# Attention and a gated convolution on one core: 1/z turned on VectorE, scaled values transposed, twelve more groups by DMA, another beginning and end

## The chip, the cores and the metric

The kernel runs on one core of a Trainium2 chip. The time is the device time of one execution in microseconds (us); three executions of the kernel before took 1075.22, 1075.74 and 1079.62 us, median 1075.74. The engines are named as in the profile: PE (TensorE), PEld (its weight loads), DVE (VectorE), ACT (ScalarE), POOL (GpSimd), SP (SyncE, which here only issues DMAs; SPq is its queue).

## The reference

Inputs are q of 4 x 12288 x 128, kv of 4 x 384 x 32 x 128 and a few matrices of 128 columns.

```python
kv_pool = kv.reshape(B, H // r, r, W // r, r, C).mean(axis=(2, 4))   # r = 4: 768 keys a batch
k = v = kv_pool.reshape(B, -1, C) @ w_sr
s = (q @ k.transpose(0, 2, 1)) / sqrt(C)
a = exp(s - s.max(-1)); a /= a.sum(-1) + 1e-09
x = a @ v
# gated convolution over x (5 taps, causal, per column)
gate = sigmoid(sum(conv_w[k] * shifted(x, k) for k in range(5)))
out = (gate * (x @ w_val)) @ w_out
```

All is float32. The matrices of the second half (w_val, w_out and the taps, one array w_moe) arrive as float64 and are turned into float32 bit by bit on DVE (14 steps, `load_moe`).

## The kernel before, in words

The host hands q, kv and the output over transposed, channels on partitions. The work is cut into 4 batches of 24 **groups** of 512 queries, and each group into four **tiles** j = 0 to 3 of 128 queries: 96 groups, 384 steps.

**Keys.** kv of a batch comes in 16 pieces of 128x768 (`load_kv`, L117) through a ring of AHEAD buffers. DVE sums each over its 4x4 blocks (`pool_kv`, L120). Two projections by w_sr (`project`, L133, 384 keys each) and three evictions (`split_keys`, L142, L143 on ScalarE, L146 on DVE) give a high part kh, a rest kl and the full vt. For the values, `column_scale` (L162 to L170) takes the largest value of each channel, makes a power of two of it and puts it on a diagonal matrix; `values` (L176) multiplies vt by this diagonal, which transposes and scales in one matmul, three tiles of 128 at a time, and L185 and L188 split the result into 16-bit vh and vl.

**One group.** A tile's score (`score`, L251) is the sum of three products kh·qh, kl·qh and kh·ql, each in two halves of 384 keys, in a pair of PSUM banks. There are three such pairs. DVE takes the row maximum (L257), ACT the exponential and its sum into a column of z (`expo`, L269), ACT the high 16-bit half of the result (`p_hi`, L316), DVE the low half (`p_lo`, L320), which is the last to read the banks. The tile must then be transposed for the product with the values. For tiles j < by_dma this is done by DMA_TRANSPOSE from SP (L324, two tiles at a time or one); for the others PE turns the float32 tile with six transposes back into its own banks (`turn`, L299) ahead of the two halves. by_dma is 3, but 4 in the even groups of the last batch. The 18 products with the values (L333, 16-bit) fill the av bank in four parts.

**1/z.** After the fourth tile ScalarE adds 1e-9 to the four sums (`norm_eps`, L273). A group later DVE takes the reciprocal (L276), PE transposes a 128x128 tile of which four columns count (`norm_turn`, L279, into the misc bank), DVE copies the four rows out (L286), one DMA stores them to DRAM (`norm_store`, L287, rd), and a second reads them back as one row on all 128 partitions (`norm_rows`, L292, rb). x is av times the power of two times rb (`g_x`, L350).

**After x.** Four taps and the sums run on POOL (L360, L369), the fifth tap on ACT (L358), the gate's tanh on ACT (L385), h on DVE (L394), and PE multiplies by w_val (L389) and w_out (L399).

**Order.** It is written by hand and nothing reorders it. In step (group, j) the program works on several groups: the scores one tile ahead, softmax of the current group `cur`, 1/z of `last` (one back), av of `avg` (two back), the convolution of `xg` (three back), the products of `mg` (four back), the store of `og` (five back). Preparing the next batch is dripped into groups 2 to 22 of the one before it and groups 0 and 1 of its own: pieces and poolings in groups 2 to 18, projections in 19 and 20, the column scale from 21, the values in the new batch's groups 0 and 1. After the last step an epilogue (L536 on) finishes the five groups in flight, written out line by line; there the convolution of the last two groups runs on DVE alone (`conv_dve`, L375, L377).

Of the kernel before, what the change touches and what calls it, by code (L numbers as in the profile page):

```python
# [17 lines left out]
GQ = 512  # L18
NT = GQ // P

# [6 lines left out]
def attn_moe_kernel(ctx, tc, qT, kvT, w_sr, w_moe, outT):  # L27
# [16 lines left out]
    AHEAD = 5  # L44
# [22 lines left out]
    zs = [const.tile([P, P], F32, name=f"z{i}") for i in range(3)]  # L67
# [55 lines left out]

    def key_tiles(st):
# [7 lines left out]
    def project(st, h, m):  # L132
        nc.tensor.matmul(m[:, :HALF], wsr, st["pool"][:, h * HALF:(h + 1) * HALF],  # L133
                         start=True, stop=True)
        st["m"] = m[:, :HALF]

    def split_keys(st, h):
        sl = slice(h * HALF, (h + 1) * HALF)
# [13 lines left out]
    def column_scale(st):  # L152
# [6 lines left out]
        st["diag"] = keys.tile([C, C], F32, name="diag", bufs=1)  # L159
# [9 lines left out]
            lambda: v.tensor_scalar_mul(out=st["diag"], in0=ident, scalar1=up.bitcast(F32)),  # L169
# [3 lines left out]
    def values(st, h, m):  # L173
        for j in range(HALF // P):
            k = h * HALF + j * P
            nc.tensor.matmul(m[:, j * P:(j + 1) * P], st["vt"][:, k:k + P], st["diag"],  # L176
                             start=True, stop=True)
        st["m"] = m[:, :HALF]
# [22 lines left out]
    def setup_steps(b, st):  # L201
# [10 lines left out]
        steps += [lambda h=h: project(st, h, misc()) or split_keys(st, h) for h in range(2)]  # L212
# [32 lines left out]
    def score(g, j):  # L245
        sl = slice(j * P, (j + 1) * P)
        kh, kl = g.st["kh"], g.st["kl"]
        s = bank_pair()
        for i, (a, k) in enumerate(((g.qh, kh), (g.qh, kl), (g.ql, kh))):
            for h in range(2):  # L250
                nc.tensor.matmul(s[:, h, :HALF], a[:, sl], k[:, h * HALF:(h + 1) * HALF],  # L251
                                 start=(i == 0), stop=(i == 2))
        g.s[j] = s[:, :, :HALF]
# [24 lines left out]
    def norm_turn(g, m):  # L278
        nc.tensor.transpose(m[:, :P], g.z, ident)  # L279
        g.rm = m[:NT, :P]  # L280

    def norm_store(g):

        r = small.tile([NT, P], F32, name="r")
        g.rd = dram.tile([NT, P], F32, name="rd")
        nc.vector.tensor_copy(out=r, in_=g.rm)  # L286
        nc.sync.dma_start(out=g.rd, in_=r)  # L287

    def norm_rows(g):
        g.rb = work.tile([C, GQ], F32, name="rb", bufs=3)  # L290
        row = g.rd.rearrange("(o j) p -> o (j p)", o=1)
        nc.sync.dma_start(out=g.rb, in_=row.broadcast_to([C, GQ]))  # L292
# [80 lines left out]
    def conv_dve(g, c0=0, c1=GQ):  # L373
# [61 lines left out]
    key_tiles(st)  # L435
    for i in range(AHEAD):
# [3 lines left out]
    g_qh(at(0))  # L440
    g_ql(at(0))
# [179 lines left out]
```

## Time and profile before

| | |
|---|---|
| three executions | 1075.22, 1075.74, 1079.62 us |
| profiled execution | 1078.68 us |
| its span | 1076.9 us, granted TensorE clock 0.996 |
| PE, DVE, ACT, POOL busy | 1038.4, 919.5, 903.7, 865.2 us |
| first and last sum of a group (L273) | 37.1 and 1050.4 us |
| queue of SP: kv, q, out, rb, rd, transposes | 64, 49, 51, 96, 96, 192 issues |

Busy time is the sum over an engine's instructions, with overlaps counted once. PE's matmuls are pipelined, so the durations of neighbours overlap; a price of one is better read from the starts. A row "a:b c, ..." of the windows gives the stretch in us, its length, and then for each engine its busy time and its count of instructions, the granted clock of PE, the busy share of the DMA engines and what they moved. In a row of the timeline the first number is the start, the second the duration; what stands in brackets is how long the engine sat idle ahead of it and what released it. Three numbers with slashes are minimum, median and maximum in ns.

### The profile page before, as it was taken

The page shows a single profiled execution, that of the slowest core. Times are in us where ns is not written, and L with a number is a line of the kernel's source. Part 1 is how long each engine was busy: PE and PEld are TensorE (multiplying, and loading weights), DVE is VectorE, ACT ScalarE, POOL GpSimd, SP SyncE. Part 2 cuts the span into 40 slices and gives each one's busy share as a digit, 9 for nine tenths or more (in the row PEclk, how much of TensorE's full clock was granted, in tenths as well). Part 3 has the DMA queues.
Part 4 walks back from the last instruction along what each step waited for, and adds up shares of the span by engine and source line. Part 5 has one row for each costly group of instructions (what it writes and reads, how often), then busy time and mean ns, then how long its engine had stood idle before and what let it go on. Part 6 is the DMA issues. An engine that isn't in the chain of part 4 may idle for free.

```text
span 1076.9 us, 16475 instructions
## 1 busy us (share of the span) xinstructions
PE 1038.4 (96%) x5102; PEld 706.5 (66%) x5102; DVE 919.5 (85%) x1290; ACT 903.7 (84%) x1659; POOL 865.2 (80%) x948
## 2 busy tenths in 40 slices
PE   1899999999999999999999999999999999999996
PEld 0666666666666666666676666666666666666663
DVE  6888989898888898988888989898888888888885
ACT  1788888888888888888888888888888988888882
POOL 0178888888888888888888888888887888888882
PEclk9999999999999999999999999999999999999999
DMA  7699999998889999999689999997899999999994
GB/s 285 115 237 215 214 225 234 200 192 190 182 186 234 226 222 224 220 214 188 156 182 221 248 216 219 235 218 177 174 203 191 200 209 218 206 194 212 201 178 120
DMA packets 505527, 220.25 MB, mean 205 GB/s; under 512 B 471520, under 2 KB 472288, under 8 KB 505440
## 3 DMA queue, kind: packets, MB, share of 16 engines
q1 hardware_dynamic: 505440, 219.20, 92.7%
q8 instruction: 41, 0.67, 0.2%
q14 instruction: 46, 0.38, 0.1%
HBM read 75.83 MB, written 25.36 MB: 94 GB/s over the span
## 4 chain that ended last, share of the span: by engine, by line
PE 89%; DVE 5%; ACT 2%; DMA 2%; issue 1%; POOL 0%; SPq 0%; DVEq 0%; ACTq 0%
PE s L251 36%; PE av L333 32%; PE m L389 7%; PE m L399 7%; PE s L299 5%; DMA kvt<-in_kv 2%; DVE nm L257 1%; PE m L279 1%; ACT s L269 1%; ACT hl L316 1%; DVE hl L320 1%; DVE pt L320 1%; DVE pool L120 0%; DVE x L350 0%; PE m L176 0%
## 5 line engine op out<-in xcount | busy, mean ns | idle before, releaser
L333 PE MATMUL av<-pt,vh 128*128 128x512 f16 x1140 | 387.1, 381 | 0.0
L369 POOL TENSOR_TENSOR sum<-sum,tap 128x512 f32<-128x512 f32 x282 | 360.3, 1278 | 22.1
L257 DVE TENSOR_REDUCE nm<-s 128x1 f32<-128x768 f32 x384 | 363.9, 948 | 2.8 <-PE s L251 2.8
L269 ACT ACTIVATE s<-s,nm 128x768 f32<-128x768 f32 x300 | 262.0, 873 | 88.7 <-DVE nm L257 80.0
L360 POOL TENSOR_SCALAR tap<-x,wm 128x512 f32<-128x512 f32 x376 | 253.4, 693 | 78.1 <-DVE x L350 76.8
L320 DVE SCALAR_TENSOR_TENSOR hl<-s,hl 128x768 f16<-128x768 f32 x300 | 284.8, 949 | 21.4 <-ACT hl L316 21.1
L251 PE MATMUL s<-kh,qh 128*128 128x384 f32 x768 | 252.9, 410 | 6.0 <-DVE hl L320 2.3
L316 ACT ACTIVATE hl<-s 128x768 f16<-128x768 f32 x300 | 243.0, 810 | 9.1
L333 PEld LDWEIGHTS <-vh 128*128 128x128 f16 x1164 | 113.5, 98 | 173.6 <-issue 81.5
L333 PE MATMUL av<-pt,vl 128*128 128x512 f16 x570 | 216.0, 379 | 0.0
L251 PE MATMUL s<-kh,ql 128*128 128x384 f32 x768 | 198.0, 339 | 0.0
L251 PE MATMUL s<-kl,qh 128*128 128x384 f32 x768 | 197.7, 338 | 0.0
L237 POOL TENSOR_TENSOR ql<-q,qh 128x512 fp32r<-128x512 f32 x96 | 122.0, 1271 | 93.3 <-ACT qh L233 92.5
L251 PEld LDWEIGHTS s<-kh,qh 128*128 128x128 f32 x768 | 132.4, 192 | 51.1 <-PE m L279 4.4
L251 PEld LDWEIGHTS s<-kl,qh 128*128 128x128 f32 x768 | 140.5, 189 | 0.5 <-DVE kl L146 0.5
L251 PEld LDWEIGHTS s<-kh,ql 128*128 128x128 f32 x768 | 139.8, 189 | 0.0
L394 DVE SCALAR_TENSOR_TENSOR h<-th,m 128x512 f32<-128x512 f32 x94 | 64.7, 688 | 69.0 <-PE m L389 63.4
L369 POOL TENSOR_TENSOR sum<-tap,tap 128x512 f32<-128x512 f32 x94 | 120.3, 1280 | 0.0
L350 DVE SCALAR_TENSOR_TENSOR x<-av,down,rb 128x512 f32<-128x512 f32 x95 | 71.3, 751 | 44.5 <-POOL ql L237 30.5
L333 PEld LDWEIGHTS <-vl 128*128 128x128 f16 x582 | 57.2, 98 | 76.6 <-issue 53.6
L399 PE MATMUL m<-h,wm 128*128 128x512 f32 x188 | 96.8, 597 | 1.2 <-DVE h L394 1.2
L389 PE MATMUL m<-x,wm 128*128 128x512 f32 x188 | 96.1, 592 | 0.0
(68 smaller groups left out, 1001.9 us busy)
## 6 DMA issues: line engine op xcount, KB each, us to landing
kvt<-in_kv SPq DMA_DIRECT2D x64, 384.0 KB
rb<-rd SPq DMA_DIRECT2D x96, 256.0 KB
q<-in_q SPq DMA_DIRECT2D x47, 512.0 KB
out<-o SPq DMA_DIRECT2D x46, 512.0 KB
pt<-hl SPq DMA_TRANSPOSE x192
rd<-r SPq DMA_DIRECT2D x96, 2.0 KB
out<-o SPq DMA_DIRECT2D x3, 256.0 KB
q<-in_q SPq DMA_DIRECT2D x2, 256.0 KB
```

The source lines that it names most:

```text
L237: nc.gpsimd.tensor_tensor(out=g.ql, in0=g.q, in1=g.qh.bitcast(F32), op=ALU.subtract)
L251: nc.tensor.matmul(s[:, h, :HALF], a[:, sl], k[:, h * HALF:(h + 1) * HALF], start=(i == 0), stop=(i == 2))
L257: nc.vector.tensor_reduce(out=nm, in_=g.s[j], axis=AX.XY, op=ALU.max, negate=True)
L269: nc.scalar.activation(out=halves(g.pf[j]) if on_pe(g, j) else g.s[j], in_=g.s[j], func=AF.Exp, bias=g.nm.pop(j), accum_out=g.z[:, j:j + 1])
L316: nc.scalar.activation(out=part(g, j, 0), in_=g.s[j], func=AF.Copy, scale=2.0 ** 15)
L320: nc.vector.scalar_tensor_tensor(out=part(g, j, 1), in0=g.s.pop(j), scalar=2.0 ** 15, in1=part(g, j, 0), op0=ALU.mult, op1=ALU.subtract)
L333: nc.tensor.matmul(out, g.st[v][:, k * P:(k + 1) * P], g.pt[:, j0:j1, a * NCH + k], start=(i == 0), stop=(i == len(AV_ORDER) - 1))
L350: nc.vector.scalar_tensor_tensor(out=g.x[:, HALO + c0:HALO + c1], in0=av, scalar=g.st["down"], in1=g.rb[:, c0:c1], op0=ALU.mult, op1=ALU.mult)
L360: eng.tensor_scalar(out=g.tap[k], in0=src, scalar1=w, scalar2=1.0, op0=ALU.mult, op1=ALU.mult)
L369: nc.gpsimd.tensor_tensor(out=s, in0=acc, in1=g.tap[k], op=ALU.add)
L389: nc.tensor.matmul(m, wval, g.x[:, HALO + c0:HALO + c1], start=True, stop=True)
L399: nc.tensor.matmul(m, wout, h, start=True, stop=True)
```

## The change

- **1/z.** z becomes 128x32. DVE takes the reciprocal and transposes it itself in 32x32 blocks into r of 128x32: each block of 32 queries leaves its four rows on partitions 0, 32, 64 and 96 on. Four DMAs of 4x32 store them in place of one of 4x128. Reciprocal and transpose now come behind the low half of the step, and PE and the misc bank have no part in it. `norm_store` and `norm_rows` take the queue as an argument.
- **Values.** The diagonal is gone. ScalarE multiplies vt by the power of two in place (128x768), and PE only transposes vt.
- **by_dma** is 4 also in groups 0, 18, 20 and 22 of the first three batches, the even ones that load no piece of keys.
- **Beginning.** w_moe is loaded first and converted by DVE first (before: dripped into the steps from the fourth on). AHEAD is 7. Pieces 0, 2, 4 and 6 are summed on POOL by four halvings each. The keys are projected in three parts (384, 288, 96 columns), each as soon as its pieces are there, in the misc bank. The first halves of the scores of tiles 0 to 2 are multiplied as soon as the first 384 keys are split.
- **End.** All of av of the last but one group comes first; rb of it is issued in step 2 of the last group, ahead of that group's transposes; rd and rb of the last group go through ScalarE's queue; the convolution of the last two groups has two of its taps on ACT (`conv_mixed`) and two adds more on DVE; products and outputs come in another order.

```diff
-    AHEAD = 5
+    AHEAD = 7
-    zs = [const.tile([P, P], F32, name=f"z{i}") for i in range(3)]
+    zs = [const.tile([P, BLOCK], F32, name=f"z{i}") for i in range(3)]
+    def pool_halving(st, i):
+        t = st.pop(("kv", i)).rearrange("c (k s) -> c k s", s=RR)
+        n = RR // 2
+        while n:
+            to = t[:, :, :n]
+            if n == 1:
+                to = st["pool"][:, i * PC:(i + 1) * PC].rearrange("c (k s) -> c k s", s=1)
+            nc.gpsimd.tensor_tensor(out=to, in0=t[:, :, :n], in1=t[:, :, n:2 * n], op=ALU.add)
+            t, n = to, n // 2
...
-            lambda: v.tensor_scalar_mul(out=st["diag"], in0=ident, scalar1=up.bitcast(F32)),
+            lambda: nc.scalar.activation(out=st["vt"], in_=st["vt"], func=AF.Copy,
+                                         scale=up.bitcast(F32)),
...
-            nc.tensor.matmul(m[:, j * P:(j + 1) * P], st["vt"][:, k:k + P], st["diag"],
-                             start=True, stop=True)
+            nc.tensor.transpose(m[:, j * P:(j + 1) * P], st["vt"][:, k:k + P], ident)
...
-    def norm_turn(g, m):
-        nc.tensor.transpose(m[:, :P], g.z, ident)
-        g.rm = m[:NT, :P]
-    def norm_store(g):
-        r = small.tile([NT, P], F32, name="r")
+    def norm_turn(g):
+        g.r = small.tile([P, BLOCK], F32, name="r")
+        nc.vector.transpose(out=g.r, in_=g.z)
+    def norm_store(g, eng):
         g.rd = dram.tile([NT, P], F32, name="rd")
-        nc.vector.tensor_copy(out=r, in_=g.rm)
-        nc.sync.dma_start(out=g.rd, in_=r)
+        for i in range(0, P, BLOCK):
+            eng.dma_start(out=g.rd[:, i:i + BLOCK], in_=g.r[i:i + NT])
...
+    def conv_mixed(g, c0, c1):
+        def product(k):
+            t = kvp.tile([C, PC * RR], F32, name="kvt", bufs=AHEAD)[:, :c1 - c0]
+            nc.scalar.activation(out=t, in_=g.x[:, k + c0:k + c1], func=AF.Copy,
+                                 scale=cwt[:, k:k + 1])
+            return t
+        late = [product(k) for k in range(TAPS - 2, TAPS)]
...
-        for k in range(1, TAPS):
+        for k in range(1, TAPS - 2):
             nc.vector.scalar_tensor_tensor(out=s, in0=g.x[:, k + c0:k + c1],
                                            scalar=cwt[:, k:k + 1], in1=s,
                                            op0=ALU.mult, op1=ALU.add)
+        for t in late:
+            nc.vector.tensor_tensor(out=s, in0=s, in1=t, op=ALU.add)
...
-            g.by_dma = 4 if b == B - 1 and i % 2 == 0 else 3
+            g.by_dma = 4 if i % 2 == 0 and (b == B - 1 or not 0 < i <= PIECES + 1) else 3
...
+    convert = load_moe()
     for i in range(AHEAD):
         load_kv(0, st, i)
...
+    by_pool = (0, 2, 4, 6)
+    ends = {PIECES // 2: slice(0, HALF), PIECES - 2: slice(HALF, NK - 2 * PC),
+            PIECES: slice(NK - 2 * PC, NK)}
+    for step in convert:
+        step()
+        if i in ends:
+            project(st, ends[i], misc())
+            high, low = split_keys(st, ends[i])
             high()
+        if i == PIECES // 2 + 1:
+            for j in first:
+                score(at(0), j, (0,))
...
-        if last and j == 0:
-            norm_reciprocal(last)
         if last and j == 1:
-            norm_store(last)
+            norm_store(last, nc.sync)
+        if cur is groups[-1] and j == 2:
+            norm_rows(last, nc.sync)
...
         if last and j == 0:
-            norm_turn(last, misc())
+            norm_reciprocal(last)
+            norm_turn(last)
-        if last and j == 3:
-            norm_rows(last)
+        if last and nxt and j == 3:
+            norm_rows(last, nc.sync)
```

Where instructions move, three places. **PE in the middle of the run**, from the last av matmul of a first part to the next score: L279 is z, L251 (after: L264) the score. Before:

```order
L333 MATMUL av<-pt,vh 128x512
L279 MATMUL m<-ident,z_101 128x128
L251 MATMUL s<-kh,qh 128x384 x2
L251 MATMUL s<-kl,qh 128x384 x2
L251 MATMUL s<-kh,ql 128x384 x2
```

After:

```order
L345 MATMUL av<-pt,vh 128x512
L264 MATMUL s<-kh,qh 128x384 x2
L264 MATMUL s<-kl,qh 128x384 x2
L264 MATMUL s<-kh,ql 128x384 x2
L411 MATMUL m<-x,wm 128x512
```

The score now follows av directly; the last row is the next product by w_val, which stood there before too.

**DVE in the same place**, from x of one group (L350, after L362) to the second low half of the next (L320, after L332). Before:

```order
L350 SCALAR_TENSOR_TENSOR x<-av,down,rb 128x512
L257 TENSOR_REDUCE nm<-s 128x1
L276 RECIPROCAL z_101<-z_101 128x4
L320 SCALAR_TENSOR_TENSOR pt<-s,pt 128x768
L257 TENSOR_REDUCE nm<-s 128x1
L286 COPY r<-m 4x128
L320 SCALAR_TENSOR_TENSOR hl<-s,hl 128x768
```

After:

```order
L362 SCALAR_TENSOR_TENSOR x<-av,down,rb 128x512
L269 TENSOR_REDUCE nm<-s 128x1
L332 SCALAR_TENSOR_TENSOR pt<-s,pt 128x768
L288 RECIPROCAL z_101<-z_101 128x4
L293 STREAM_TRANSPOSE r<-z_101 128x32
L269 TENSOR_REDUCE nm<-s 128x1
L332 SCALAR_TENSOR_TENSOR hl<-s,hl 128x768
```

The reciprocal has gone behind the low half, the transpose stands next to it, and nothing stands between the second row maximum and the second low half.

**SP in the last two groups**: rd and rb are the two steps of 1/z, L324 (after L336) the transposes of the last group's tiles. Before:

```order
L287 DMA rd<-r 4x128
L324 DMA_TRANSPOSE pt<-hl 128x24x128
L324 DMA_TRANSPOSE pt<-hl 128x12x128
L292 DMA rb<-rd 128x512
L287 DMA rd<-r 4x128
L413 DMA out<-o 128x1024
L292 DMA rb<-rd 128x512
```

After:

```order
L299 DMA rd<-r 4x32 x4
L304 DMA rb<-rd 128x512
L336 DMA_TRANSPOSE pt<-hl 128x24x128
L336 DMA_TRANSPOSE pt<-hl 128x12x128
L435 DMA out<-o 128x1024
```

The first rb has passed both transposes; the last rd and rb are no longer on this queue. In the middle of the run the order on SP is as before, with four rows of rd for one.

More of the change, by code (lines that the diff above doesn't have):

```diff
@@ L130, in key_tiles, with project, split_keys @@
         st["vt"] = keys.tile([C, NK], F32, name="vt", bufs=1)
-    def project(st, h, m):
-        nc.tensor.matmul(m[:, :HALF], wsr, st["pool"][:, h * HALF:(h + 1) * HALF],
-                         start=True, stop=True)
-        st["m"] = m[:, :HALF]
-    def split_keys(st, h):
-        sl = slice(h * HALF, (h + 1) * HALF)
+    def project(st, sl, m):
+        m = m[:, :sl.stop - sl.start]
+        nc.tensor.matmul(m, wsr, st["pool"][:, sl], start=True, stop=True)
+        st["m"] = m
+    def split_keys(st, sl):
         m = st.pop("m")
@@ L243, in halves, with score @@
         return a.rearrange("p (h k) -> p h k", h=2)
-    def score(g, j):
+    def score(g, j, part=range(2)):
         sl = slice(j * P, (j + 1) * P)
         kh, kl = g.st["kh"], g.st["kl"]
-        s = bank_pair()
+        if j not in g.s:
+            g.s[j] = bank_pair()[:, :, :HALF]
         for i, (a, k) in enumerate(((g.qh, kh), (g.qh, kl), (g.ql, kh))):
-            for h in range(2):
-                nc.tensor.matmul(s[:, h, :HALF], a[:, sl], k[:, h * HALF:(h + 1) * HALF],
+            for h in part:
+                nc.tensor.matmul(g.s[j][:, h], a[:, sl], k[:, h * HALF:(h + 1) * HALF],
                                  start=(i == 0), stop=(i == 2))
-        g.s[j] = s[:, :, :HALF]
     def row_max(g, j):
@@ L439, in attn_moe_kernel @@
     nc.sync.dma_start(out=wsr, in_=w_sr)
-    g_qh(at(0))
-    g_ql(at(0))
+    first = range(3)
+    by_pool = (0, 2, 4, 6)
+    ends = {PIECES // 2: slice(0, HALF), PIECES - 2: slice(HALF, NK - 2 * PC),
+            PIECES: slice(NK - 2 * PC, NK)}
     low = None
-    for i in range(PIECES):
-        if i + AHEAD < PIECES:
-            load_kv(0, st, i + AHEAD)
-        if i == 3:
-            convert = load_moe()
-        pool_kv(st, i)
-        if i == 3 * PIECES // 4:
-            low()
-        if i % (PIECES // 2) == PIECES // 2 - 1:
-            h = 2 * i // PIECES
-            project(st, h, bank_pair()[:, 0])
-            high, low = split_keys(st, h)
+    for step in convert:
+        step()
+    for i in range(1, PIECES + 1):
+        if i - 1 + AHEAD < PIECES:
+            load_kv(0, st, i - 1 + AHEAD)
+        (pool_halving if i - 1 in by_pool else pool_kv)(st, i - 1)
+        if low and i - 1 in ends:
+            low()
+        if i == PIECES // 2:
+            g_qh(at(0))
+            g_ql(at(0))
+        if i in ends:
+            project(st, ends[i], misc())
+            high, low = split_keys(st, ends[i])
             high()
+        if i == PIECES // 2 + 1:
+            for j in first:
+                score(at(0), j, (0,))
     low()
@@ L541, in attn_moe_kernel, with pair_of @@
     cuts = ((0, half), (half, GQ))
-    def bank():
-        return bank_pair()[:, 0]
+    def pair_of(width):
+        both = bank_pair()
+        return both[:, 0, :width], both[:, 1, :width]
+    for i in range(NT):
+        av_part(n2, i)
     norm_reciprocal(n1)
-    av_part(n2, 0)
-    norm_turn(n1, misc())
+    norm_turn(n1)
+    norm_store(n1, nc.scalar)
     n4.th = g_tanh(n4.gate)
```

73 lines of the change are left out of this document (35 added, 38 removed).

## The prediction

> **What bounds the kernel now.** I read the busy times and the chain of waits first.
>
> ```profile
> PE 1038.4 (96%) x5102; PEld 706.5 (66%) x5102; DVE 919.5 (85%) x1290; ACT 903.7 (84%) x1659; POOL 865.2 (80%) x948
> PE 89%; DVE 5%; ACT 2%; DMA 2%; issue 1%; POOL 0%; SPq 0%; DVEq 0%; ACTq 0%
> ```
>
> TensorE is busy for 96% of the span, and 89% of the chain that ended last is its work. But a mean over 1077 us hides stages, so I cut the time at the last softmax sum of a group (the scaling of z on ScalarE, once a group) and read the windows between such marks.
>
> ```profile
> L273 ACT ACTIVATE z<-z x96: 205/206/207, 37.1 to 1050.4; 128x4 f32<-128x4 f32 x96
> core 0: us, PE busy (x) PEld busy (x) DVE busy (x) ACT busy (x) POOL busy (x), PEclk, DMA share, GB/s
> 37.08:47.53 10.45, 7.15 (x38) 5.88 (x37) 9.37 (x19) 8.13 (x16) 1.30 (x2) 0.95 0.61 113
> 47.53:57.83 10.30, 9.76 (x54) 6.86 (x55) 10.09 (x19) 8.19 (x15) 1.39 (x2) 1.00 1.06 193
> 463.73:484.95 21.22, 21.22 (x108) 14.59 (x106) 19.14 (x27) 18.65 (x34) 18.37 (x21) 1.00 0.88 199
> 977.91:998.80 20.89, 20.80 (x103) 13.94 (x101) 17.49 (x24) 18.54 (x34) 18.32 (x21) 1.00 1.05 206
> 550.66:573.30 22.64, 22.64 (x120) 16.00 (x118) 18.51 (x26) 19.20 (x37) 18.34 (x21) 1.00 0.79 180
> ```
>
> Four limits show. Ahead of 37.1 us the first keys are made. In groups 1 and 2 (rows two and three) VectorE is nearly full (10.09 of 10.30) and TensorE is not. From then on a pair of groups takes 21.22 us with TensorE busy all of it (20.89 in the last batch, whose even groups turn no tile on TensorE; 22.64 where two sets of values are made). After 1050.4 us comes a tail of 26.5 us that is one chain. So a TensorE instruction taken away between 60 and 1050 us should come off the time in full, as long as the next engine (VectorE, 19.14 of 21.22) stays behind.
>
> **1/z without TensorE.** The durations of matmuls overlap, so a price is a difference of starts.
>
> ```profile
> 479.77 0.38 PE L333 MATMUL av<-pt,vl 128*128 128x512 f16 x1
> 479.99 0.38 PE L333 MATMUL av<-pt,vh 128*128 128x512 f16 x1
> 480.55 0.51 PE L251 MATMUL s<-kl,qh 128*128 128x384 f32 x2
> 487.91 0.59 PE L333 MATMUL av<-pt,vh 128*128 128x512 f16 x2
> 488.82 0.34 PE L251 MATMUL s<-kl,qh 128*128 128x384 f32 x1
> 484.90 0.38 PE L333 MATMUL av<-pt,vh 128*128 128x512 f16 x1
> 485.12 0.82 PE L299 MATMUL s<-ident,pf 128*128 128x128 f32 x6
> 486.12 0.34 PE L251 MATMUL s<-kl,qh 128*128 128x384 f32 x1
> ```
>
> From the last av matmul to the first kl product it is 0.56 us with nothing between (479.99 to 480.55). With the z transpose between it is 0.69 (the second of the two av starts 0.22 after 487.91, at 488.13, and kl at 488.82): 0.13. With the six transposes of a tile it is 1.22, so 0.66 more, 0.11 each. I take 0.11 for the z transpose, times the 92 or so groups that TensorE bounds: −10 us; 0.13 gives −12.
>
> VectorE pays for it. It loses the copy (0.271 us) and gains a transpose of 128x32, which the trace does not have.
>
> ```profile
> L286 DVE COPY r<-m 4x128 f32<-4x128 f32 x96 | 26.0, 271 | 1.1
> L299 PE MATMUL s<-ident,pf 128*128 128x128 f32 x504 | 69.6, 275 | 1.2 <-ACT pf L269 1.1
> L176 PE MATMUL m<-diag,vt 128*128 128x128 f32 x48 | 6.9, 280 | 0.4 <-ACT o L409 0.4
> L316 ACT ACTIVATE hl<-s 128x768 f16<-128x768 f32 x300 | 243.0, 810 | 9.1
> L96 DVE TENSOR_TENSOR rest<-rest 128x261 int32<-128x261 int32 x3 | 1.2, 404 | 0.0
> ```
>
> Its bounds: nothing more than the copy, and the 0.947 us of a whole reduction of 128x768, the longest VectorE step. A 32-column step is nearest the small copy, so I take no change; at the upper bound VectorE has 19.14 − 0.54 + 1.9 = 20.5 of a pair of 21.0, still behind TensorE. The Trainium skill ("VectorE: DVE Perf Modes", section "The three transpose paths") gives 311 ns for a 128x128 bf16 transpose in 32x32 blocks on VectorE; no run here shows that yet, and by it the term would not change.
>
> **Twelve more groups wholly by DMA.** Each drops six transposes, 0.66 us. But the trace of the last batch shows that less comes back.
>
> ```profile
> 959.07 0.93 DVE L320 SCALAR_TENSOR_TENSOR hl<-s,hl 128x768 f16<-128x768 f32 x1
> 959.78 0.27 PE L279 MATMUL m<-ident,z 128*128 128x128 f32 x1
> 960.11 0.30 PEld L251 LDWEIGHTS s<-kh,qh 128*128 128x128 f32 x2 [0.40 <-PE m L279]
> ```
>
> Here, after a DMA-only group, TensorE is through with av and z at about 959.8 and starts the next score at 960.1: that score's banks are read by this low-half step, which ends at 960.00. So the pair gains 21.22 − 20.89 = 0.33. Eleven of the twelve (group 0 is counted below): 11 × −0.3 = −3.3; from 0 (the bank wait grows) to −7.3 (it vanishes). In the changed order the reciprocal stands behind the low half instead of ahead, which pulls this wait in by some 0.09 us.
>
> **Values.** 48 matmuls are two for each of 24 tiles, since a float32 product is issued twice; a transpose is one (504 = 84 × 6). Each of eight sets of three tiles sheds three of 0.11: −0.33 for the six after the first batch, −2 us. ScalarE takes one 128x768 scaling more per batch (0.81, by the same shape) in a pair where it has 18.65 of 21.22; VectorE drops the diagonal. If the scaling lands ahead of a high half that TensorE waits for, it costs up to 0.8 × 3 = 2.4; I take nothing.
>
> **The beginning.**
>
> ```profile
> 22.67 0.95 DVE L120 TENSOR_REDUCE pool<-kvt 128x48 f32<-128x768 f32 x1 [0.80 <-DMA kvt<-in_kv]
> 23.68 1.65 PE L133 MATMUL s<-pool,wsr 128*128 128x384 f32 x2 [7.82 <-DVE pool L120]
> 25.37 0.49 ACT L142 ACTIVATE kh<-s 128x384 fp32r<-128x384 f32 x1 [8.60 <-PE s L133]
> 26.27 0.56 DVE L146 SCALAR_TENSOR_TENSOR kl<-s,kh 128x384 fp32r<-128x384 f32 x1 [2.64 <-ACT vt L143]
> 28.25 0.96 DVE L257 TENSOR_REDUCE nm<-s 128x1 f32<-128x768 f32 x1 [1.42 <-PE s L251]
> ```
>
> The last pooling waits for its transfer, so loading sets 22.67, and a larger AHEAD or pooling on GpSimd moves it by a microsecond at most; w_moe, now first on SP, holds the keys back by about as much. From the last pooling's end (23.62) to the first row maximum it is 4.6 us: a projection of 384 columns, two copies, a difference, six products. With 96 columns last and first halves already multiplied, the projection (1.65) goes to a quarter, high and low likewise, and three of six products are gone: about 2.5 less, between 1.5 and 3.5. Then w_moe's conversion (4.9 us of VectorE in 14 steps like the one at L96, all in groups 1 and 2) goes ahead into the load, where VectorE waits; group 0 turns no tile; and 2 × 0.33 of values go. These groups lie between VectorE and ScalarE (8.13), so not all of 4.9 comes back: −3, from −1 to −4. If the conversion delayed the first poolings by its 4.9, the loads would wait on buffers and the start would gain nothing; seven buffers instead of five cover that.
>
> **The end.**
>
> ```profile
> 1048.45 5.19 SPq L324 DMA_TRANSPOSE pt<-hl  x2
> 1053.73 0.84 SPq L292 DMA_DIRECT2D rb<-rd  x1
> 1053.73 4.14 DMA rb<-rd
> 1058.01 0.75 DVE L350 SCALAR_TENSOR_TENSOR x<-av,down,rb 128x512 f32<-128x512 f32 x1 [4.73 <-POOL sum L369]
> 1055.27 3.95 POOL L369 TENSOR_TENSOR sum<-sum,tap 128x512 f32<-128x512 f32 x3
> 1059.00:1060.00 1.00, 1.00 (x2) 0.48 (x3) 0.96 (x3) 0.00 (x0) 0.22 (x1) 0.50 0.41 94
> ```
>
> The last but one group's x waits for rb, whose issue stands behind two transposes on SP. Put ahead, rb goes when the four rd have landed, about 1051, and x comes at 1055.2: −2.8. The transposes then go some 3 us later, but their group is wanted only behind x. Two of five taps leave VectorE for ScalarE and TensorE's last av is ahead of the gates: −1 to −2. TensorE still pauses for rb, and the granted clock may fall to 0.50 as at 1059. I take −4.5, from 0 (the late transposes eat it) to −6.5.
>
> **Four rd for one.** SP issues three more per group.
>
> ```profile
> L287 SPq DMA_DIRECT2D rd<-r x96: 260/282/642, 42.1 to 1054.6; - x96
> L292 SPq DMA_DIRECT2D rb<-rd x96: 319/840/1657, 50.7 to 1057.2; - x96
> 954.59 4.09 SPq L324 DMA_TRANSPOSE pt<-hl  x1
> 972.67 0.54 SPq L222 DMA_DIRECT2D q<-in_q  x1
> ```
>
> In this pair of the last batch SP works through ten instructions between 954.59 and 973.21 with one pause of 0.7 at 959.3, 18 us of 20.9 with the gaps of 0.09; six more at 0.28 + 0.09 make 20.2. It just fits: I take nothing. Queued behind the rd on SP are the next transposes and rb, and av waits for those.
>
> **Sum.** −2.5 − 3 − 10 − 3.3 − 2 − 4.5 = −25.3 on this execution of 1078.68 us (span 1076.9, 1.8 around it), which lies 2.9 above the median of the timed runs, 1075.74: 1050.4 us, rounded 1050.5.
>
> **Rivals.**
> 1. *Another bound takes over.* VectorE's low halves free the three score buffers in turn, and after DMA-only groups TensorE already waits for one. If that holds in all groups, the z transpose comes off only in part (0.09 of 0.11 after DMA-only groups at best, nothing elsewhere), and start, end and values remain: −12 to −15, 1061 to 1064. Against it: 21.22 of 21.22 busy. 17%.
> 2. *The end returns its gain.* The page "SBUF — State Buffer" of the Trainium skill, section "SBUF: two separate sides", says that a VectorE step with two SBUF inputs and a GpSimd step reading SBUF exclude each other. No row here has such a pair in the end, since the first tap with two inputs starts after the last sum (1059.22). As a mechanism of this kernel: the new gate of the last but one group has four steps with two SBUF inputs from about 1056 on, beside three sums of 1.3 that now end at 1059.2; waiting for these costs 1.3 to 3.8. With late transposes the end gives nothing: 1052 to 1055. 15%.
> 3. *SP saturates* (the other side). The pair above has room for (20.7 − 18) / 6 = 0.45 us per added issue. At the longest of the row, 0.64 + 0.09, six more make 22.4 of 20.9: +1.5 a pair, 18 in the last batch, and the new DMA-only groups gain nothing (3.3): −25.3 + 21.3, near 1072. At the median of the other issue that touches rd, 0.84 + 0.09, they make 23.6, +2.7 a pair or 32, and the 36 earlier pairs, at about 16 to 17 of 21.2 by the same count, come to 22 and lose some 0.9 each, 32: −25.3 + 32 + 3.3 + 32 = +42, near 1118. The middle is 1090; it is slower than before from 0.75 us per issue on. For it: 128-byte rows are new. Against it: the median of 0.28, with the same number of bytes in all. 8%, of which 5 lie beyond 0.75.
>
> **Numbers.** My forecast has 60%. 0.5% is about what a measurement of this kernel can tell from no change, 5.4 us. Forecast, 1 and 2 all lie below 1070.4 (92%); a part of rival 3 falls within, and some of 1 may: faster 0.90, same 0.05, slower 0.05. Range: 1044 (turn at 0.13, start and end at their good bounds) to 1063 (rival 1).
>
> **What would show it.** Pairs of groups in mid-run at 21.0 us or less, TensorE still full, confirm the z term; 21.2 with TensorE waiting for a low half says rival 1. Pairs with a new DMA-only group should fall by 0.3 more. The first row maximum should come at 25 to 26 us, the fourth group's sum 5 us earlier than before, x of the last but one group 2.8 us nearer to the last sum, and the tail be 22 us. Gaps of TensorE ahead of av in the last batch, with SP never idle, would say rival 3. A transpose on VectorE of more than 1 us would make the z term wrong.

## The result, and the profile after

The changed kernel takes 1070.68 us (median of 5 executions, 1068.99 to 1071.81); the kernel before took 1077.02 beside it (5 executions, 1075.22 to 1079.62). The ratio is 0.9938, 95% interval 0.9926 to 0.9951: 6.3 us faster, where 25 were predicted. The profiled execution has a span of 1067.2 us, 9.7 less than that of before. Each of the two profiles is 1.7 us off its kernel's median, on opposite sides, so the spans exaggerate the gain; what follows in pieces is worked out on them.

The page of after, busy times and chain of waits:

```profile
PE 1021.7 (96%) x4912; PEld 686.6 (64%) x4912; DVE 918.1 (86%) x1283; ACT 910.6 (85%) x1671; POOL 874.5 (82%) x964
PE 74%; DVE 11%; ACT 9%; POOL 2%; issue 2%; DMA 2%; SPq 0%; DVEq 0%; ACTq 0%; POOLq 0%
```

TensorE lost 16.7 us of work and is as full as before (96% of the span), but the chain that ends last is now TensorE's for 74% and not 89%: other engines have come into it. Next the view of the line of the last sum of a group (after: L285), and the window of the same pair of groups as in the prediction, columns as there:

```profile
L285 ACT ACTIVATE z<-z x96: 205/206/206, 37.7 to 1038.9; 128x4 f32<-128x4 f32 x96
core 0: us, PE busy (x) PEld busy (x) DVE busy (x) ACT busy (x) POOL busy (x), PEclk, DMA share, GB/s
461.89:482.84 20.95, 20.95 (x102) 14.05 (x101) 19.17 (x27) 18.48 (x35) 18.36 (x21) 1.00 0.96 211
L293 DVE STREAM_TRANSPOSE r<-z x96: 211/212/216, 41.3 to 1039.7; 128x32 f32<-128x32 f32 x96
```

The pair fell from 21.22 to 20.95 with TensorE busy all of it, and VectorE's transpose takes 0.212 us, under the copy that it replaces. So the middle does what was said. The two marks cut the span in three:

| stretch | before | after | difference | predicted |
|---|---|---|---|---|
| to the first sum | 37.1 | 37.7 | +0.6 | −3.4 |
| four groups behind it | 40.9 | 39.9 | −0.9 | −2.1 |
| from there to the last sum | 972.4 | 961.2 | −11.2 | −15.3 |
| last sum to the end | 26.5 | 28.3 | +1.8 | −4.5 |

(The prediction gives its early term, −3, as one; the split into 0.9 to the first sum and 2.1 behind it is made here. The mark of the first sum moves by up to 1 us between profiles of the same beginning: it is 37.1 before and 36.1 in experiment 5.) In the third stretch the usual group fell by 0.137, but some groups are irregular: 11.66, 10.83, 11.06, 11.04 us where their kind takes 10.47 or 10.21. Below, the **irregular part** of a profile is what its groups, from the fifth on and without the last three, take beyond the median of their kind in that profile, added up: 4.4 us here, against 0.8 before. This timeline of after shows the longest one, TensorE, VectorE and SP; below it stand two rows of the views of waits (total, times, longest) and the row of the four rd:

```profile
106.46 0.45 SPq L304 DMA_DIRECT2D rb<-rd  x1
107.43 1.34 SPq L299 DMA_DIRECT2D rd<-r  x4
111.18 0.75 DVE L362 SCALAR_TENSOR_TENSOR x<-av,down,rb 128x512 f32<-128x512 f32 x1 [1.51 <-DMA rb<-rd]
111.98 0.38 PE L345 MATMUL av<-pt,vh 128*128 128x512 f16 x1 [0.72 <-DVE x L362]
DVE x L362 <- DMA rb<-rd: 5.1, 5, 1.7
SPq L336 <- DMA rb<-rd: 24.8, 23, 2.3
L299 SPq DMA_DIRECT2D rd<-r x380: 243/321/1596, 43.3 to 1038.1; - x190
```

rb is issued 4.72 us ahead of the moment when x starts; x waits 1.51 for it to land, and TensorE, which needs the av bank that x reads, 0.72. Between 60 and 1035 us there are five such waits of x, none in the kernel before, and 23 times a transpose on SP stands until an rb has landed. Of the four groups named, 11.66 and 11.04 hold such a wait of x; in the group of 11.06 TensorE's av waits 0.44 for a transpose by DMA, and for 10.83 the profile shows neither. The four rd take 0.32 us each in the median, up to 1.6. From rb's issue to x it was 8.2 us in the median before, and 6.3 after.

The beginning of after, VectorE, and SP's loads from the eighth on:

```profile
5.92 0.76 DVE L97 TENSOR_TENSOR rest<-rest 128x261 int32<-128x261 int32 x1
10.63 2.67 DVE L121 TENSOR_REDUCE pool<-kvt 128x48 f32<-128x768 f32 x3
25.51 0.46 DVE L157 SCALAR_TENSOR_TENSOR kl<-m,kh 128x288 fp32r<-128x288 f32 x1 [1.30 <-ACT vt L154]
25.88 0.94 DVE L121 TENSOR_REDUCE pool<-kvt 128x48 f32<-128x768 f32 x1
29.44 1.92 DVE L269 TENSOR_REDUCE nm<-s 128x1 f32<-128x768 f32 x2 [1.10 <-PE s L264]
11.60 5.58 SPq L118 DMA_DIRECT2D kvt<-in_kv  x9
```

From the end of the last pooling to the first row maximum it is 2.6 us where it was 4.6: the three projections and the early first halves give 2.0. But the last pooling starts at 25.88 and not at 22.67. The conversion holds VectorE until 10.6, so buffers come free late (the eighth load goes out at 11.60; before, at 7.87), and VectorE waits 1.30 us for a copy (kl of the second part) that stands ahead of the last pooling.

The end of after, VectorE and ScalarE (ACTq is ScalarE's DMA queue):

```profile
1043.82 0.75 DVE L362 SCALAR_TENSOR_TENSOR x<-av,down,rb 128x512 f32<-128x512 f32 x1 [2.21 <-PE av L345]
1045.76 0.36 ACTq L304 DMA_DIRECT2D rb<-rd  x1
1046.15 0.19 ACT L358 COPY x<-x 128x4 f32<-128x4 f32 x1 [3.21 <-DMA rd<-r]
1046.38 0.49 DVE L395 TENSOR_SCALAR fast<-x,wm 128x512 f32<-128x512 f32 x1 [1.81 <-ACT x L358]
1046.90 2.43 DVE L397 SCALAR_TENSOR_TENSOR fast<-x,wm,fast 128x512 f32<-128x512 f32 x2
1052.63 0.48 DVE L362 SCALAR_TENSOR_TENSOR x<-s,down,rb 128x256 f32<-128x256 f32 x1 [1.71 <-PE s L345]
```

x of the last but one group comes 4.9 us behind the last sum; it was 7.65. Then it is lost: ScalarE stands 3.2 us in the wait for rd ahead of the last rb, and the copy and the two taps that VectorE needs are queued behind it. Two taps take 2.43 us, in part beside GpSimd's last sums (until 1048.0), and the first half of the last x waits for the second half's av too.

### The profile page after: what moved, and what is told of

Same layout as the page of the kernel before. It is cut to its first block, busy times and chain, and to the rows that moved or that the text cites. A ratio compares the mean times of both kernels' runs of the same rounds, so it can differ in the third digit from the quotient of the medians.

```text
span 1067.2 us, 16368 instructions
## 1 busy us (share of the span) xinstructions
PE 1021.7 (96%) x4912; PEld 686.6 (64%) x4912; DVE 918.1 (86%) x1283; ACT 910.6 (85%) x1671; POOL 874.5 (82%) x964
## 4 chain that ended last, share of the span: by engine, by line
PE 74%; DVE 11%; ACT 9%; POOL 2%; issue 2%; DMA 2%; SPq 0%; DVEq 0%; ACTq 0%; POOLq 0%
PE s L264 30%; PE av L345 25%; PE m L411 7%; PE m L421 5%; PE s L311 4%; ACT s L281 4%; DVE nm L269 3%; ACT hl L328 2%; DVE h L416 2%; POOL ql L248 2%; DVE x L362 1%; DVE hl L332 1%; ACT qh L244 1%; DMA rb<-rd 1%; PE m L146 1%
## 5 line engine op out<-in xcount | busy, mean ns | idle before, releaser
L281 ACT ACTIVATE s<-s,nm 128x768 f32<-128x768 f32 x312 | 272.5, 873 | 76.9 <-DVE nm L269 73.3
L332 DVE SCALAR_TENSOR_TENSOR hl<-s,hl 128x768 f16<-128x768 f32 x312 | 296.9, 952 | 23.8 <-ACT hl L328 23.6
L264 PE MATMUL s<-kh,qh 128*128 128x384 f32 x768 | 257.0, 415 | 8.1 <-DVE pw L174 2.1
L328 ACT ACTIVATE hl<-s 128x768 f16<-128x768 f32 x312 | 252.6, 810 | 9.1
L264 PE MATMUL s<-kl,qh 128*128 128x384 f32 x768 | 198.8, 339 | 0.3 <-DVE kl L157 0.3
L264 PE MATMUL s<-kh,ql 128*128 128x384 f32 x768 | 198.8, 339 | 0.0
L264 PEld LDWEIGHTS s<-kh,qh 128*128 128x128 f32 x768 | 137.8, 191 | 65.8 <-issue 29.1
L264 PEld LDWEIGHTS s<-kl,qh 128*128 128x128 f32 x768 | 140.7, 190 | 0.8 <-DVE kl L157 0.7
L264 PEld LDWEIGHTS s<-kh,ql 128*128 128x128 f32 x768 | 140.5, 190 | 0.0
L362 DVE SCALAR_TENSOR_TENSOR x<-av,down,rb 128x512 f32<-128x512 f32 x95 | 71.3, 751 | 46.8 <-POOL ql L248 28.7
L345 PEld LDWEIGHTS <-vl 128*128 128x128 f16 x582 | 57.1, 98 | 77.7 <-issue 54.5
```

What stands on the lines that cost most here:

```text
L264: nc.tensor.matmul(g.s[j][:, h], a[:, sl], k[:, h * HALF:(h + 1) * HALF], start=(i == 0), stop=(i == 2))
L281: nc.scalar.activation(out=halves(g.pf[j]) if on_pe(g, j) else g.s[j], in_=g.s[j], func=AF.Exp, bias=g.nm.pop(j), accum_out=g.z[:, j:j + 1])
L328: nc.scalar.activation(out=part(g, j, 0), in_=g.s[j], func=AF.Copy, scale=2.0 ** 15)
L332: nc.vector.scalar_tensor_tensor(out=part(g, j, 1), in0=g.s.pop(j), scalar=2.0 ** 15, in1=part(g, j, 0), op0=ALU.mult, op1=ALU.subtract)
L345: nc.tensor.matmul(out, g.st[v][:, k * P:(k + 1) * P], g.pt[:, j0:j1, a * NCH + k], start=(i == 0), stop=(i == len(AV_ORDER) - 1))
```

## The experiments

The ratios compare with the kernel before, run beside each experiment on the same chip. Diffs are against the changed kernel unless said.

**1. One DMA for 1/z.** The sums stand in columns 0, 8, 16 and 24 of z, so the 16 rows of r lie 8 partitions apart and go in one DMA.

```diff
-        for i in range(0, P, BLOCK):
-            eng.dma_start(out=g.rd[:, i:i + BLOCK], in_=g.r[i:i + NT])
+        eng.dma_start(out=g.rd.rearrange("j (i c) -> i j c", c=BLOCK), in_=g.r[::STEP])
```

> The changed kernel, but the four rows of 1/z go to DRAM in one DMA of 16 rows of 128 bytes instead of four of four rows (the sums stand 8 columns apart, so that one step over the partitions picks them). Theory A, the four issues delay rb: from the issue of rb to x there were 7.2 to 9.4 us before and only 4.0 to 8 with the change, and a landing takes 4.1; the groups over 10.6 us in which TensorE waits for x (11.66, 10.83, 11.06, 11.04 and smaller ones, some 4 us in all) should vanish, rb go back to more than 7 us ahead of x, and the time fall by 3 to 5 us, to a ratio of about 0.990. Theory B, these groups are chance of the transfers and not of the issues: they stay, and the time stays at a ratio of 0.994.

Measured: 1064.48 us (1064.42 to 1064.66), ratio 0.9873, 0.9858 to 0.9888. The irregular part of the groups fell from 4.4 to 1.4 us, rb to x rose to 7.6 in the median, and the executions agree within 0.3 us where they spread over 2.8. Waits of x and the row of rd on SP:

```profile
DVE x L362 <- DMA rb<-rd: 1.4, 2, 0.7
L299 SPq DMA_DIRECT2D rd<-r x95: 525/542/675, 43.5 to 1033.8; - x95
```

Theory A, and 6.2 us (7.0 by the two ratios) are more than it asked for: in this pair of profiles the tail is 2.4 us shorter as well (rb of the last group goes out 5.2 us behind the last sum instead of 6.9). That part varies: with this end, four profiles with four rd have tails of 26.4, 26.4, 28.3 and 29.7 (experiments 3 and 13, the change, 2), five with this one rd 25.9 to 26.3. Against this kernel, whose times hardly spread, the other terms can be read better.

**2. The old rule for by_dma** (3 tiles but in the last batch).

> The changed kernel with the old rule for by_dma: groups 0, 18, 20 and 22 of the first three batches turn their fourth tile on TensorE again. As predicted, each would cost 0.3, some 3.3 us more in all (ratio 0.997). Theory A, read from the trace after: only groups behind 18 and 22 are shorter (0.26 and 0.13), behind 20 and 0 TensorE waits 0.8 us for the misc bank, which ScalarE empties, instead of turning, so undoing costs 1.2 us in the spans between the sums and no more. Against it, theory B: SP has less to do with one transpose fewer in each of these groups, fewer late rb, so undoing may gain 1 us.

Measured: 1078.30 us (1076.10 to 1081.09), ratio 1.0002, 0.9990 to 1.0014. Neither: 7.6 us slower (6.9 by the ratios). Its profile has an irregular part of 8.2 us; the regular part of the loss is 2.9 us. The irregular groups are the wait of the change again, more often: rb to x is 5.6 us in the median (6.3 in the change), and x waits for rb 18 times between 60 and 1045 us.

```profile
DVE x L362 <- DMA rb<-rd: 14.1, 18, 1.5
```

**3. The old beginning.**

> The changed kernel with the beginning of before (poolings all on VectorE, two projections, five buffers, w_moe loaded after nine pieces and converted between the steps). Theory A: the new beginning costs, since the first row maximum came at 29.44 instead of 28.25: it goes back to 28.3 and the first sum to 36.3 (8.27 of group 0 with no turned tile, or up to 0.6 more since the first halves are no longer multiplied ahead); but the conversion is back in groups 1 and 2, which took 0.24 and 0.90 less without it, so in all the time is the same within 1 us. Theory B, as predicted: the new beginning and early groups save 5.5 us, so undoing them costs that.

Measured: 1071.96 us, ratio 0.9941, 0.9922 to 0.9960, against 0.9938: the same. First sum at 36.2, the four groups behind it 41.6. Theory A: what the new beginning loses ahead of the first sum, the early groups give back (77.8 us to the mark behind the four groups here, 77.7 in the change).

**4. The old end.**

> The changed kernel with the end of before (rb of the last but one group behind the transposes on SP, rd and rb of the last group on SP, all five taps on VectorE, halves of av in banks of their own, the old order of outputs). Theory A, read from the trace after: from the last sum to the end it is 28.3 us now and was 26.5, so undoing it saves 1.8 us. Theory B, as predicted: the new end saves 4.5 and the longer tail is due to something else (the clock, the transfers): undoing it costs, and the tail is over 29.

Measured: 1073.07 us, ratio 0.9961, 0.9944 to 0.9978. Inconclusive: the tail of its profile is 1.2 us shorter, but with four rd the irregular groups (8.5 us in its profile) hide a term of this size.

**5. Four rd in the kernel before**, nothing else.

```diff
-        nc.sync.dma_start(out=g.rd, in_=r)
+        for i in range(0, P, P // 4):
+            nc.sync.dma_start(out=g.rd[:, i:i + P // 4], in_=r[:, i:i + P // 4])
```

> The kernel before with one thing changed: the 4x128 row of 1/z goes to DRAM in four DMAs of 4x32 instead of one of 4x128. TensorE's and VectorE's work is untouched. Theory A, four issues on SP make rb late: rb to x falls from a median of 8.2 us to about 6, groups of 11 us and more appear at random, some 4 to 8 us in all, and the ratio is 1.004 to 1.008. Theory B, the gain of the single DMA in the first experiment came from its end or from something else in it: the ratio is 1.000 within 0.002, and the groups stay at 10.61.

Measured: 1078.35 us, ratio 1.0004, 0.9993 to 1.0015; irregular part 0.5 us. Theory A fell in this form: four issues alone cost nothing that shows (by the interval at most 1.6 us), though the transposes wait for rb here too:

```profile
SPq L325 <- DMA rb<-rd: 26.1, 22, 1.7
```

So in the kernel before neither the issues as such nor these waits cost time. I then counted, from the timeline of SP, how long its queue is idle per group (gaps over 0.12 us between DMA instructions; groups 4 to 18 of the second batch, and groups 2 to 20 of the last):

| kernel | second batch | last batch | rb to x, median |
|---|---|---|---|
| before | 2.4 | 1.8 | 8.2 |
| before, four rd (5) | 1.1 | 0.3 | 7.1 |
| after | 0.7 | 0.3 | 6.3 |
| after, one rd (1) | 1.3 | 1.0 | 7.6 |

Before the change, an SP queue almost without idle time still brought rb early enough. With groups that are 0.14 shorter and transposes that take 3.1 us to issue and not 2.9 or 3.0 (means, groups 4 to 18 of the second batch), it did not.

**6. One rd and the old rule for by_dma** (1 and 2 together).

> The single-DMA kernel of the first experiment with the old rule for by_dma (groups 0, 18, 20 and 22 of the first three batches turn a tile on TensorE). With the disturbance of the four DMAs gone the term can be read: group 19 goes back from 10.22 to 10.47, group 23 from 9.70 to 10.41, groups 21 and 1 stay (TensorE waits there for the misc bank instead), so 0.96 a batch, 2.9 us in all, ratio 0.990. Theory B, from the second experiment, where the same edit cost 7.6 us: transposes on TensorE do something to the transfers as well, and it costs 7 us here too, ratio 0.994.

Measured: 1068.42 us, ratio 0.9922, 0.9905 to 0.9938; 3.9 us slower than 1, as A to within a microsecond, and group 19 is back at 10.47, group 23 at 10.41, groups 21 and 1 of the later batches unchanged. The rest of the 3.9 is not in these groups: group 1 of the whole run takes 1.3 more in this profile than in that of 1, and it varies from 9.9 to 12.1 between all profiles. With four rd the same edit cost 7.6, and rb came later still there (experiment 2); why it did, with fewer transposes on SP, stays open.

**7. One rd, conversion spread over the later poolings.** w_moe is loaded after seven pieces; two steps of the conversion behind each pooling from the ninth on; kl of the second part behind the last pooling.

```diff
-    for step in convert:
-        step()
...
-        if low and i - 1 in ends:
+        if i > PIECES // 2:
+            for step in convert[:2]:
+                step()
+            convert = convert[2:]
+        if i in (PIECES // 2 + 1, PIECES):
             low()
```

> The single-DMA kernel of the first experiment with another order in the beginning: w_moe is loaded after the first seven pieces, its conversion runs two steps behind each pooling from the ninth piece on instead of ahead of all poolings, and the rest of the second projection is taken behind the last pooling. Theory A, the conversion ahead of the poolings keeps buffers from being freed (the eighth load went out at 11.60 us) and the last pooling waited 1.3 us behind a copy: the last pooling starts at 23 to 24 instead of 25.9, the first row maximum comes at 26.5 instead of 29.4, the early groups stay, and the time falls by 2 to 3 us, ratio 0.985. Theory B, loading alone sets the beginning: the last pooling stays at 25 or later, and the time within 0.5 us.

Measured: 1065.54 us, ratio 0.9889, 0.9874 to 0.9903: no gain. But not by theory B's reason. VectorE's last pooling and the DMA share of this run:

```profile
25.71 0.95 DVE L122 TENSOR_REDUCE pool<-kvt 128x48 f32<-128x768 f32 x1
22.00:26.00 4.00, 1.33 (x2) 0.50 (x2) 3.93 (x10) 0.71 (x2) 0.00 (x0) 1.00 0.01 3
```

Loading is over by 22 us; VectorE is the late one (3.93 of 4 busy), with the conversion now among the last poolings. Behind the halvings the 14 steps take 4.9 us again, about as in the kernel before.

**8. One rd, three moves in the end.**

```diff
-    norm_rows(n1, nc.scalar)
-    avs = pair_of(half)
+    avs = [bank_pair()[:, 0, :half] for _ in cuts]
...
     gate2 = conv_mixed(n2, 0, GQ)
+    norm_rows(n1, nc.scalar)
...
-    g_out(g_h(n3.th, m3), o3)
     g_val(n1, ms[1], *cuts[1])
+    g_out(g_h(n3.th, m3), o3)
```

> The single-DMA kernel of the first experiment with three things moved in the end: rb of the last group is issued behind the last but one group's taps on ScalarE and not ahead of them, the two halves of the last av have banks of their own, and the second half's product by w_val stands ahead of the third group's last product. Theory A, these waits set the tail: VectorE's idle time ahead of the first half's x and of the last h (1.7 us) goes, the tail falls from 25.9 to 23.5 or 24 us after the last sum, ratio 0.985. Theory B, VectorE's own work in the tail and GpSimd's sums beside it set the end (its two taps with two inputs take 1.65 us each beside them, 0.78 alone): the tail falls by less than 1 us.

Measured: 1062.30 us, ratio 0.9860, 0.9845 to 0.9874, 2.2 us under 1; the tail of its profile is 24.7 against 25.9, so 1.2 of it; most of the rest lies ahead of the first sum (36.9 against 37.8), where the program is the same, so it is not the edit's. Between the two theories: the waits went, and VectorE is now busy without a gap from 1041 to 1054. Its two taps beside GpSimd's sums in this run, and the same form alone in the kernel before (four):

```profile
1041.96 3.32 DVE L397 SCALAR_TENSOR_TENSOR fast<-x,wm,fast 128x512 f32<-128x512 f32 x2
```

```profile
1059.79 3.11 DVE L377 SCALAR_TENSOR_TENSOR fast<-x,wm,fast 128x512 f32<-128x512 f32 x4
```

That is 1.66 us each against 0.78.

**9. 1/z on TensorE again, the rest of the change kept** (one rd of 4x128; the reciprocal ahead of the low half again; six buffers instead of seven, for want of room).

> The changed kernel with 1/z turned on TensorE and copied by VectorE again, and one rd of 4x128 (six buffers for the keys instead of seven, for want of room). Against the single-DMA kernel of the first experiment this undoes the 1/z term alone. Theory A, as predicted and as the groups show (10.61 before, 10.47 after, where nothing else differs): 0.137 for each of some 75 groups and 0.07 behind DMA-only groups, 11 us, ratio 0.9975, with groups of 10.61 again. Theory B, VectorE's chain of low halves already held TensorE, and the shorter groups come from elsewhere (the reciprocal behind the low half): half of it, ratio 0.992.

Measured: 1076.45 us, ratio 0.9990, 0.9980 to 0.9999; 12 us slower than 1, and 9.9 of them lie between the first and the last sum. Theory A.

```profile
L285 ACT ACTIVATE z<-z x96: 205/205/206, 38.5 to 1047.3; 128x4 f32<-128x4 f32 x96
```

```profile
L286 ACT ACTIVATE z<-z x96: 210/211/213, 37.8 to 1036.8; 128x4 f32<-128x4 f32 x96
```

(The first row is this kernel, the second experiment 1.) The usual group is 10.61 again. It also says that all the rest of the change, with one rd, is worth about a microsecond.

**10. One rd, the scaling of vt in four pieces.**

> The single-DMA kernel of the first experiment with ScalarE's scaling of vt cut into four pieces of 128x192, one in each of four steps, for the last three batches. Groups 22 and 23 take 11.83 and 9.70 now; with the scaling whole it stands ahead of a high half, and TensorE waits 0.62 and 0.79 for banks. Theory A, it is the length of the piece: the two groups together fall from 21.53 to 21.0 or less, 1.5 us in three batches. Theory B, ScalarE's total in these groups sets them: no change.

Measured: 1064.37 us, ratio 0.9877, 0.9862 to 0.9891, the same as 1. Groups 22, 23 and the next 0 take 11.35, 10.32 and 10.41 instead of 11.83, 9.70 and 10.47, in sum the same. Theory B, for the two groups together even 0.1 more; what in them sets the sum was not taken apart further.

**11. One rd, four tiles by DMA in groups 18 and 22 only.**

> The single-DMA kernel of the first experiment with four tiles by DMA only in groups 18 and 22 of the first three batches, no longer in 0 and 20. Theory A, behind 20 and 0 TensorE stands 0.8 us at the misc bank (projection, values) for ScalarE's eviction, so that no turned tile there changes nothing: groups 21 and 1 stay at 11.17 and 10.81, the time the same as with all four (ratio 0.987), but for group 0 of the whole run. Theory B, as predicted, each gives 0.3: 1.5 to 2 us slower.

Measured: 1065.12 us, ratio 0.9883, 0.9868 to 0.9897; groups 21 and 1 at 11.18 and 10.81, as with all four. Theory A. TensorE and the eviction that it waits for, in after and then in this kernel, both at group 20's end:

```profile
247.70 0.58 ACT L431 ACTIVATE o<-m 128x512 f32<-128x512 f32 x1
248.33 0.91 PE L146 MATMUL m<-pool,wsr 128*128 128x384 f32 x2 [0.42 <-ACT o L431]
```

```profile
246.34 0.58 ACT L431 ACTIVATE o<-m 128x512 f32<-128x512 f32 x1
246.39 0.82 PE L311 MATMUL s<-ident,pf 128*128 128x128 f32 x6
247.04 0.85 PE L147 MATMUL m<-pool,wsr 128*128 128x384 f32 x2
```

The projection starts 0.63 and 0.70 us behind the eviction's start in the one and the other: the turned tile was done in time that TensorE would have stood anyway.

**12. One rd, conversion in VectorE's early gaps, the end of 8, the scaling of 10.**

> The single-DMA kernel with a beginning whose conversion fills VectorE's early gaps (w_moe loaded third, two steps behind each of the first poolings, none from the ninth piece on), the end of the eighth experiment, and the scaling in four pieces. Theory A, VectorE's backlog at the last pieces (last pooling at 25.7 with loads through at 22) made the beginning late: the last pooling starts at about 23, the first row maximum at 27 instead of 29.5; with 1.2 of the end and 1.5 of the scaling the time is about 1058 to 1059, ratio 0.983. Theory B, the beginning stays where it was: 1061, ratio 0.985.

Measured: 1061.57 us, ratio 0.9849, 0.9834 to 0.9864. Nearer to B: first row maximum at 28.3. Two steps of the conversion, the first while GpSimd halves, the second while it makes ql; then the same forms in the kernel before, without such neighbours (count | busy us, mean ns | idle):

```profile
10.25 0.96 DVE L95 TENSOR_SCALAR rest<-rest 128x261 int32<-128x261 int32 x1
15.47 1.27 DVE L98 TENSOR_TENSOR rest<-rest 128x261 f32<-128x261 f32 x1
```

```profile
L93 DVE TENSOR_SCALAR rest<-rest 128x261 int32<-128x261 int32 x1 | 0.3, 275 | 0.0
L96 DVE TENSOR_TENSOR rest<-rest 128x261 f32<-128x261 f32 x1 | 0.4, 409 | 0.0
```

Not every step is stretched: the next single-input step of the conversion (at 11.13) takes 0.28 beside the same halving, and the poolings keep their 0.94. In all the 14 steps take 7.4 us here and 4.9 in experiment 7, so GpSimd's help with the poolings is paid for in part by VectorE.

**13. Four rd, but rb on ScalarE's queue.**

```diff
-            norm_rows(last, nc.sync)
+            norm_rows(last, nc.scalar)
```

> The changed kernel, four rd as they are, but rb of each group is issued on ScalarE's queue (same step) and no longer behind the transposes on SP. Theory A, the four issues hurt because SP's queue is full (idle 0.5 us a group, 0.1 in the last batch, against 2.4 and 1.7 before) and rb stands at its end: with rb elsewhere it goes out some 3 us earlier, the irregular groups vanish, and the time comes to that of the single-DMA kernel, 1064 to 1066, if ScalarE bears an issue of 0.4 to 0.9 us a group (it has 9.4 of 10.5). Theory B, the short rows disturb the transfers themselves: irregular groups stay and the time is 1070 or more.

Measured: 1063.79 us, ratio 0.9869, 0.9854 to 0.9884. Theory A: rb goes out 11.6 us behind the sum (median) instead of 15.0, no x waits for rb any more, and the four short rows stay. So the short rows as such are not what cost 6 us; rb behind a full queue is. The edit does two things at once, though: it takes rb out of its place, and it takes one issue per group off SP, whose idle time rises to 1.1 and 0.5. The waits of x (18 in experiment 2, five in the change, none here) speak for the place; no run separates the two.

**14. One rd, the end of 8, of the new beginning only the three projections, the early first halves and seven buffers**; all poolings on VectorE, w_moe converted between the steps as before.

> The single-DMA kernel with the end of the eighth experiment and, of the new beginning, only the three projections, the first halves of the scores ahead and seven buffers: all poolings are on VectorE and w_moe's conversion is dripped into groups 1 and 2 as before. Theory A, what made the beginning late is VectorE's work ahead of the last pooling (the conversion, slowed by GpSimd's halvings): the last pooling starts at 22.7 as before, the first row maximum comes at 26.3 (2.6 behind the pooling's end), groups 1 and 2 take 0.2 and 0.9 longer, and the time is 2 to 3 us under the eighth experiment's 1062.3, near 1060. Theory B, more buffers and parts don't move the last pooling or it is slower without GpSimd: the first row maximum is at 28 or later, time 1063.

Measured: 1059.87 us (1058.60 to 1060.65), ratio 0.9828, 0.9812 to 0.9845: theory A, and the fastest of all.

```profile
16.67 6.10 DVE L122 TENSOR_REDUCE pool<-kvt 128x48 f32<-128x768 f32 x7
24.93 0.26 DVE L158 SCALAR_TENSOR_TENSOR kl<-m,kh 128x96 fp32r<-128x96 f32 x1 [1.25 <-ACT vt L155]
26.29 0.96 DVE L270 TENSOR_REDUCE nm<-s 128x1 f32<-128x768 f32 x1 [1.10 <-PE s L265]
```

The seven poolings run without a gap to 22.8, and the first row maximum is at 26.3, 2 us ahead of the kernel before (1.1 ahead of experiment 3, which has the old beginning too) and 3.1 ahead of the change.

## Why the prediction was wrong, point by point

- **"1/z without TensorE", −10.** Right: 0.137 a group, a little over the two prices, 0.11 and 0.13; behind DMA-only groups only 0.07 (10.29 to 10.22); in all 9.9 us between the sums by experiment 9. VectorE's transpose at 0.212 us was inside its bounds. Rival 1 is out.
- **"Four rd for one", 0.** This step failed most: +6.2 us by experiment 1. The count of SP's work was right and "it just fits" was nearly so (experiment 5 fits). What was missing is that rb is the last thing in that queue and has a deadline: it landed 4.1 us behind its issue in the row of the prediction, and x came 6 to 10 us behind the issue, 8.2 in the median. The slack of rb, not SP's idle time, was the number to look up: with four rd and shorter groups the median fell to 6.3, the least to 3.7, and x waited. Rival 3 named the place, but its price was for a steady lack of room; in fact single groups fail. The median issue was 0.32 us, well under the 0.45 from which it was to decide.
- **"Twelve more groups wholly by DMA", −3.3.** Right in size (0.26 behind 18 and 0.71 behind 22, so 2.9 in three batches; 3.9 in all, experiment 6), wrong in place: nothing behind 20 and 0, where the misc bank sets the start.
- **"Values", −2.** Right: the six value groups of the later batches fell from 11.32 to 10.81, 0.37 each beyond the 1/z term. **The scaling, 0**, was not: groups 22 and 23 take 22.24 in experiment 6 and took 21.94, although 1/z is off. That is +0.57 a batch if 1/z came off in full there, +0.41 at the 0.11 that experiments 1 and 9 differ by in the two groups: 1.2 to 1.7 us, inside the bound of 2.4 that the prediction gave and set aside. No run puts the diagonal back alone, so that it is the scaling is argued, not shown.
- **"The beginning", −2.5 and −3.** The part behind the last pooling was right (−2.0). "Seven buffers instead of five cover that" failed: the conversion did delay the poolings, the eighth load went out at 11.60 us, and VectorE never caught up. Beside GpSimd's halvings the conversion took 7 us instead of 4.9. So +1.2 at the first row maximum; the early groups gave 1.5 of 3. Experiment 14 has what was predicted for the part that was sound.
- **"The end", −4.5.** The first piece was right: x of the last but one group came 2.7 us nearer to the last sum (2.8 predicted). "−1 to −2" for the taps failed: two taps moved to ScalarE leave two adds behind, 0.75 us each against 0.78 for a tap, so VectorE saves next to nothing. And moving rb to ScalarE's queue was priced at nothing, though ScalarE's copy and taps stand behind its wait. Rival 2 had the right mechanism: beside GpSimd's sums a tap takes 1.66 us instead of 0.78 (experiment 8). The Trainium skill, page "SBUF — State Buffer", section "SBUF: two separate sides", says that a VectorE step with two SBUF inputs and a GpSimd step that reads SBUF exclude each other; the traces agree as far as such steps took longer, 1.66 against 0.78 in the end of experiment 8 and 1.27 against 0.41 for the two-input step in experiment 12.

Worked out with one rd: start and early groups about 0 instead of −5.5, 1/z −9.9, DMA groups −2.9, values −2.2, scaling +1.2 to +1.7, end −0.6: −14.4 to −13.9, and experiment 1 measured −13.4. Four rd give 6.2 of it back.

## What to carry to other kernels

A transfer that costs the engines nothing still stands in a queue: for every DMA that a change adds, look up what is last in that queue and how many microseconds it has between its landing and its use, not only whether the queue has idle time. Work taken off the bounding engine comes back in full only where the wait behind it is not another one (here a bank that ScalarE empties), so price it at each place and not by the mean. Ahead of a loop, filling an idle engine pays only if nothing on the path is queued behind it: a conversion put "where VectorE waits" made VectorE the bound.

## What was not expected

One DMA can pick 16 rows from partitions 8 apart: 16 rows of 128 bytes take 0.54 us to issue where four issues take 0.32 each. Beside GpSimd some single-input steps on VectorE took longer too (0.96 us for a step of 0.28, experiment 12), not only those with two inputs. The kernel before spreads by 5 us from one execution to the next (1075.2 to 1080.2 over all of them), the one of experiment 1 by 0.3. Irregular groups don't explain the former, since its profile has few. In the executions beside the experiments its time goes with TensorE's granted clock: 1075.4 to 1075.8 us at 1.000, 1078.6 to 1080.2 at 0.995. But experiment 1 took 1064.4 to 1064.7 at 0.995 and at 0.998, so the cause stays open.
